# A spectral mixing kernel and its feed-forward layer: the second batch's inputs loaded before weight block 5, and two of three row loads moved to GpSimd's queue

## The chip, the cores and the metric

The kernel runs on one core of a Trainium2 chip. The time is the device time of one execution in microseconds. The kernel before took 2579.2 us in the median of three runs (2575.68 to 2580.06).

## The reference

The input x has 8 batches of 3008 positions and 256 channels. Each channel is filtered in the frequency domain, and the result goes through a feed-forward layer with 2048 hidden units, all in float32. The two weight matrices and the other inputs are given in their own types; the weights are 64-bit floats, which the kernel turns into float32 itself.

```python
X = np.fft.rfft(x, axis=1)
Y = X * (filt_r + 1j * filt_i)[None, :, :]
y = np.fft.irfft(Y, n=x.shape[1], axis=1)       # (8, 3008, 256)
t = y.reshape(8 * 3008, 256)
h = t @ w_in                                    # (24064, 2048)
out = (h * (1 / (1 + np.exp(-h)))) @ w_out      # (24064, 256)
```

## The kernel before

The main part is the feed-forward layer. It runs in 384 steps: 48 pieces of tokens by 8 pairs of hidden blocks. Each step has 14 matmuls of 128x128 by 256 (lines 756 and 819); they use a seven-product scheme, so the weights stand in SBUF in seven combinations (w_t, filled by place_weights and combine_weights). While the steps of one batch run, the Fourier transforms of the next batch are put between them by a list of due times. That list holds for everything after step 0; what comes before is written out by hand, in the order in which each engine is to do it, and the change lies there.

This opening does four things at once, because nothing can start before them:

1. Weights. load_weights (lines 926 and 929) loads block j of 16 as two DMAs of 256 KB on SP's queue. VectorE and ACT turn the 64-bit words into float32 (bits, converted, rounded) and VectorE places the products in w_t (placed). Blocks 0 to 3 are loaded first, 4 to 8 later, 9 just before the main loop.
2. Tables and filters. The transform's tables d_t, e_t and wi_t and the filters come by SP's, ACT's and POOL's queues (POOL is the profile's name of GpSimd, whose DMAs go by a queue of their own).
3. The first batch's transform: stage1_first, then for each of six groups g a forward (line 467), a product with the filters, and an inverse (line 527, matmuls into pc). rows_first (line 541) copies the two results of a group from PSUM, by ACT, and for groups 4 and 5 one of them by VectorE, and stores each with a 256-KB DMA (line 543) into a DRAM tile d2. The store is issued by the engine that copied, or by SP where VectorE copied. Twelve stores in all.
4. The transform's last stage reads d2 in another order. load_t4_rows(k) (line 571) loads part k in two DMAs of 256 KB each. Part 0 needs the stores of groups 0 and 1, part 1 of groups 2 and 3, part 2 of groups 4 and 5. The rows go to a part of w_t that the weights don't need yet. stage3(g) for g = 0 to 3 (line 586, matmuls into pd) needs all three parts, and the main loop begins with its results.

The second batch's first two pieces are also begun here: load_two loads 768 KB into x_all (line 277, SP's queue), after the first batch's stage 1 has read x_all for the last time; stage1 (line 345) multiplies it. Between this and stage 3, idle_wide(n) (line 1055) puts n matmuls whose result nobody reads.

Engines work in their own order and wait for each other by semaphores. A DMA is issued by the engine named in the call, in its order, so an issue that must wait holds up what follows on that engine.

Of the kernel before, what the change touches and what calls it, by code (L numbers as in the profile page):

```python
# [170 lines left out]
def kernel(  # L171
# [9 lines left out]
    nc = tc.nc  # L181
# [69 lines left out]
    def bank(b, name, spare=None):  # L251


        if early[0] is None and spare in ("x", "yz"):
            return xps.tile([128, 2, C], FP32, name=name, tag=spare)
        if early[0] is None and spare is not None:
            return accps.tile([128, 2, C], FP32, name=name, tag=f"a{spare}")
        if early[0] is None:
            return fps.tile([128, 2, C], FP32, name=name, tag="f")
        early[0] += 1  # L260
        k = early[0] % 8
        if k < 2:
            return fps.tile([128, 2, C], FP32, name=name, tag="f")
        if k > 5:
            return xps.tile([128, 2, C], FP32, name=name, tag="x" if k == 6 else "yz")
        return accps.tile([128, 2, C], FP32, name=name, tag=f"a{k - 2}")
# [459 lines left out]
    def combine(eng, out, in0, in1, op):  # L726
        eng.tensor_tensor(out=out, in0=in0, in1=in1, op=op)  # L727
# [176 lines left out]
    def load_weights(j, queue=None):  # L904

        if j in (8, 11, 12, 13):
            pool, tag = (t4pool, "t4") if j in (11, 12) else (upool, "u")
            raw = pool.tile([128, 2, 512], U32, name=f"raw_{j}", tag=tag)
        else:

            if j in (0, 2):
                t = ypool.tile([128, 2, HALF], FP32, name=f"raw_{j}", tag="y")
                raws.setdefault("tiles", []).append(t)
                raws["at"] = t.rearrange("p a n -> p (a n)").bitcast(U32)[:, 0:2048]
                raws["y"] = raws["at"]
                raws.setdefault("first", raws["at"])
            elif j == 4:
                raws["at"] = spool.tile([128, 2048], U32, name=f"raw_{j}", tag="s")
            elif j == 6:
                raws["at"] = gpool.tile([128, 2048], U32, name=f"raw_{j}", tag="g")  # L920
            elif j in (9, 14):
                raws["at"] = raws["y"]
            at = 1024 * (j in (1, 3, 5, 7, 10, 15))
            raw = raws["at"][:, at:at + 1024].rearrange("p (w n) -> p w n", w=2)
        queue = queue or nc.sync
        queue.dma_start(
            out=raw[:, 0].rearrange("p (a n) -> p a n", a=2),
            in_=moe_w_in.bitcast(U32)[:, 256 * j:256 * j + 256].rearrange("(a p) n -> p a n", p=128))
        queue.dma_start(out=raw[:, 1], in_=moe_w_out.bitcast(U32)[128 * j:128 * j + 128, :])
        raws[j] = raw  # L930

    def bits_of_weights(*js):

        for j in js:
            words = raws[j].rearrange("p w (n t) -> p (w n) t", t=2)
            if j in (6, 7):

                room = w_t.rearrange("p j c w n -> p (j c w n)")[:, (7168, 13056)[j - 6]:][:, 0:1024].bitcast(U32)
                e, m = room[:, 0:512], room[:, 512:1024]
            elif j in (0, 1, 4, 5):  # L940
                if "scratch" not in raws:
                    raws["scratch"] = gpool.tile([128, 4, 512], U32, name="scratch", tag="g")
                e, m = (raws["scratch"][:, 2 * (j % 2) + i] for i in range(2))
            else:
                e = zpool.tile([128, 512], U32, name=f"e_{j}", tag="z")
                m = ppool.tile([128, 512], U32, name=f"m_{j}", tag="p")
            lo, hi = words[:, :, 0], words[:, :, 1]
            ef, mf = e.bitcast(FP32), m.bitcast(FP32)
            ends = (lo, hi) if j in (2, 3, 6, 7) else (m, e)
            raws[j] = lo, hi, e, m, ef, mf, ends[0].bitcast(FP32), ends[1].bitcast(FP32), ends[1]  # L950
            v.tensor_scalar(out=e, in0=hi, scalar1=20, scalar2=0x7ff,
                            op0=ALU.logical_shift_right, op1=ALU.bitwise_and)
            v.tensor_scalar(out=m, in0=hi, scalar1=0xfffff, scalar2=None, op0=ALU.bitwise_and)
# [42 lines left out]
    def combine_weights(jp, part=None, eng=None):  # L996

        eng = eng or v

        def w(c):  # L1000
            return w_t[:, jp, c]
        if part != 1:
            combine(eng, w(S1), w(S3), w(A22), ALU.add)
            combine(eng, w(S2), w(S1), w(A11), ALU.subtract)
        if part != 0:
            combine(eng, w(S3), w(A11), w(S3), ALU.subtract)
            combine(eng, w(S4), w(A12), w(S2), ALU.subtract)

    def weights(*js, queue=None):
        for j in js:  # L1010
            if wide:
                load_weights(j, queue)

    def bits(*js):
        if wide:
            bits_of_weights(*js)
# [34 lines left out]
    def idle_wide(n, ps=None, rhs=None):  # L1051

        ps = ps or bank(0, "idle")
        for _ in range(n):
            nc.tensor.matmul(out=ps[:, 0], lhsT=wx_t, rhs=wide_rows if rhs is None else rhs,
                             start=True, stop=True)
# [4 lines left out]
    part, second = spectral(0), spectral(1)  # L1061
# [13 lines left out]
    nc.scalar.dma_start(out=d_t[:, 16:NS], in_=d_dram[:, 16:NS])  # L1075
    nc.scalar.dma_start(out=e_t[:, 2:NG], in_=e_dram[:, 2:NG])
    nc.sync.dma_start(out=wi_t, in_=ws_dram.ap())
    weights(4, 5, 6, 7)

    signed = []  # L1080
    for i in range(2):
        t = typool.tile([128, 2, 2, 2, 128], FP32, name=f"signed_{i}", tag="ty")
# [26 lines left out]
    for k in range(16):  # L1109
        part["stage1_first"](k, 2)  # L1110
        if k in whole:
            part["stage1_first"](whole[k], 3)
    second["load_two"]()
    weights(8)
    part["forward"](0, fill=4)
    placed(0, 1)
    for g in range(1, 4):
# [8 lines left out]
    def inverse(g):  # L1126
        part["inverse_first"](g)
        part["rows_first"](g)
# [15 lines left out]
    for k in range(2):  # L1144
        part["add"](NG - 1, k)
    bits(4, 5)
    inverse(4)
    combine_weights(0)
    inverse(5)
    bits(6, 7, 8)  # L1150
    for k in range(2):
        part["load_t4_rows"](k)
    part["load_t4_rows"](2)
    converted(4, 5)
    placed(2, 3)
# [11 lines left out]
    gp.tensor_copy(out=gate, in_=w_t[:, 4, A11, 0, 0:1])  # L1167
    for u in range(2):
        second["store_rows"](u)
    idle_wide(16)  # L1170
    for g in range(4):
        part["stage3"](g)
    nc.sync.dma_start(out=wi_t, in_=wi_dram.ap())
# [93 lines left out]
```

## Time and profile before

| what | value |
|---|---|
| median of three runs | 2579.2 us |
| the profiled execution | 2579.25 us |
| its span, first to last instruction | 2577.4 us |
| TensorE busy over the span | 2553.1 us, 99% |
| mean granted TensorE clock | 0.995 |
| stage 3 (line 586) of the opening starts | 69.10 us |
| first matmul of the main loop (line 756) | 76.94 us |

Busy time of TensorE counts its matmuls; PEld is its loading of weights, beside the matmuls. A "q" behind an engine's name means its issuing side. Times in the views are microseconds from the start of the span. In the windows view, a row has the stretch, its length, the busy time (and number of instructions) of TensorE, its weight loads, VectorE, ACT and POOL, then the granted clock as a share of full speed, the mean busy share of the 16 DMA engines, and GB/s moved. In the timeline, a row has start, duration, engine, line, operation, output and inputs with shapes, the number of instructions, and in brackets the idle time before and what ended it. In the chain of waits, a row has start, duration and what the chain went through.

### The profile page before, as it was taken

The page shows a single profiled execution, that of the slowest core. Times are in us where ns is not written, and L with a number is a line of the kernel's source. Part 1 is how long each engine was busy: PE and PEld are TensorE (multiplying, and loading weights), DVE is VectorE, ACT ScalarE, POOL GpSimd, SP SyncE. Part 2 cuts the span into 40 slices and gives each one's busy share as a digit, 9 for nine tenths or more (in the row PEclk, how much of TensorE's full clock was granted, in tenths as well). Part 3 has the DMA queues.
Part 4 walks back from the last instruction along what each step waited for, and adds up shares of the span by engine and source line. Part 5 has one row for each costly group of instructions (what it writes and reads, how often), then busy time and mean ns, then how long its engine had stood idle before and what let it go on. Part 6 is the DMA issues. An engine that isn't in the chain of part 4 may idle for free.

```text
span 2577.4 us, 47850 instructions
## 1 busy us (share of the span) xinstructions
PE 2553.1 (99%) x18714; PEld 2196.6 (85%) x18714; DVE 1664.4 (65%) x3589; ACT 1090.4 (42%) x3019; POOL 430.3 (17%) x688
## 2 busy tenths in 40 slices
PE   8999999999999999999999999999999999999998
PEld 6688888888888888888888888888888888888987
DVE  7766666676666666666666676666666666555554
ACT  3544444444444444444444444444444444444443
POOL 4212111111122111311121111211121112101101
PEclk9899999999999999999999999999999999999999
DMA  9522232222223222322233122331232211200011
GB/s 291 158 60 52 70 79 63 60 68 72 59 64 69 70 65 55 79 71 67 59 70 80 49 66 59 79 80 46 66 86 64 68 41 34 59 18 16 9 17 16
DMA packets 198554, 171.06 MB, mean 66 GB/s; under 512 B 122068, under 2 KB 173380, under 8 KB 197348
## 3 DMA queue, kind: packets, MB, share of 16 engines
q1 hardware_dynamic: 176056, 117.06, 19.9%
q0 software_dynamic: 17344, 45.70, 5.6%
q10 hardware_dynamic: 4928, 5.24, 0.7%
q8 instruction: 147, 2.41, 0.4%
q14 instruction: 79, 0.65, 0.1%
HBM read 96.07 MB, written 81.26 MB: 69 GB/s over the span
## 4 chain that ended last, share of the span: by engine, by line
PE 96%; DMA 2%; DVE 0%; ACT 0%; issue 0%; SPq 0%; ACTq 0%; DVEq 0%
PE acc L819 44%; PE px L756 26%; PE pyz L756 19%; PE pd L586 3%; PE pb L467 2%; PE pc L510 2%; PE pf L434 1%; DMA filt<-in_filt_i_dram 0%; PE pa L354 0%; DMA w_t<-in_x_dram 0%; DMA d_t<-d_tbl 0%; PE pa L345 0%; DMA x_all<-in_x_dram 0%; DMA d<-q 0%; DMA w_t<-d 0%; DMA t<-d 0%
## 5 line engine op out<-in xcount | busy, mean ns | idle before, releaser
L819 PE MATMUL acc<-g,w_t 128*128 128x256 f32 (+1 forms) x5376 | 1509.2, 375 | 0.4 <-DVE g L727 0.4
L819 PEld LDWEIGHTS acc<-g,w_t 128*128 128x128 f32 x5376 | 1021.6, 190 | 115.7 <-DVE g L727 0.8
L727 DVE TENSOR_TENSOR g<-pyz,abc 128x256 f32<-128x256 f32 (+1 forms) x1152 | 480.0, 417 | 621.6 <-ACT abc L777 356.2
L727 DVE TENSOR_TENSOR g<-g 128x256 f32<-128x256 f32 (+3 forms) x1152 | 599.4, 520 | 196.7 <-ACT g L760 183.5
L756 PE MATMUL px<-ty,w_t 128*128 128x256 f32 (+1 forms) x2304 | 679.4, 377 | 1.1 <-ACT abc L771 0.6
L760 ACT ACTIVATE g<-g 128x256 f32<-128x256 f32 (+1 forms) x1152 | 472.9, 410 | 250.2 <-DVE g L727 250.2
L727 POOL TENSOR_TENSOR s<-s 128x256 f32<-128x256 f32 (+1 forms) x329 | 255.0, 792 | 1417.5 <-DVE s L839 1321.0
L756 PEld LDWEIGHTS px<-ty,w_t 128*128 128x128 f32 x2304 | 432.7, 190 | 65.5 <-issue 6.2
L756 PE MATMUL pyz<-y,w_t 128*128 128x256 f32 (+1 forms) x1536 | 454.0, 377 | 0.0
L756 PEld LDWEIGHTS pyz<-y,w_t 128*128 128x128 f32 x1536 | 283.9, 190 | 47.6 <-DVE g L727 6.8
L771 ACT COPY abc<-px 128x256 f32<-128x256 f32 (+1 forms) x384 | 141.3, 368 | 372.9 <-PE px L756 372.9
L777 ACT COPY abc<-px 128x256 f32<-128x256 f32 (+1 forms) x384 | 141.5, 369 | 339.0 <-PE px L756 338.1
L760 ACT ACTIVATE g<-px 128x256 f32<-128x256 f32 (+1 forms) x384 | 145.8, 380 | 300.9 <-PE px L756 300.8
L756 PE MATMUL px<-y,w_t 128*128 128x256 f32 (+1 forms) x768 | 232.7, 385 | 0.8 <-DVE y L600 0.8
L756 PE MATMUL pyz<-ty,w_t 128*128 128x256 f32 (+1 forms) x768 | 225.8, 376 | 0.3 <-DVE g L727 0.2
L756 PEld LDWEIGHTS px<-y,w_t 128*128 128x128 f32 x768 | 140.4, 190 | 33.0 <-DVE y L606 5.3
L756 PEld LDWEIGHTS pyz<-ty,w_t 128*128 128x128 f32 x768 | 144.5, 190 | 19.2 <-DVE g L727 1.5
L764 ACT COPY abc<-px 128x256 f32<-128x256 f32 (+1 forms) x384 | 135.4, 353 | 52.7 <-PE px L756 52.7
L586 PEld LDWEIGHTS pd<-wi_t,t 48*64 48x64 f32 x3840 | 61.1, 135 | 25.1 <-ACT g L760 16.4
L446 POOL DMA_DIRECT2D d<-tf x144 | 71.6, 504 | 29.2 <-DVE tf L442 29.2
L839 ACT COPY s<-acc 128x512 f32<-128x512 f32 (+1 forms) x94 | 54.2, 577 | 47.6 <-PE acc L819 47.4
L869 DVE STREAM_TRANSPOSE o<-s 128x256 f32<-128x256 f32 x192 | 73.9, 423 | 0.4 <-issue 0.3
(136 smaller groups left out, 1269.9 us busy)
## 6 DMA issues: line engine op xcount, KB each, us to landing
t<-d SPq DMA_DIRECT2D x120, 192.0 KB
t<-d SPq DMA_DIRECT2D x84, 256.0 KB
d<-q POOLq DMA_DIRECT2D x84, 256.0 KB, 2.7
out_dram<-o SPq DMA_DIRECT2D x636, 32.0 KB
d<-tf POOLq DMA_DIRECT2D x144, 96.0 KB, 3.2
xr<-in_x_dram SPq DMA_DIRECT2D x6, 1472.0 KB
x_all<-in_x_dram SPq DMA_DIRECT2D x72, 96.0 KB
x_all<-xr SPq DMA_DIRECT2D x72, 96.0 KB
```

Source lines behind the costliest of these rows:

```text
L446: nc.gpsimd.dma_start(out=d1[k // 2, :, k % 2, n0:n0 + 4], in_=us["tf"][32 * k:32 * k + NS].rearrange("p q n c -> p (q n) c"))
L467: nc.tensor.matmul(out=ps[k][32 * j:32 * j + 32, ri, :], lhsT=d_t[rows, 4 * g + at, ri, :], rhs=rhs, start=True, stop=True)
L586: nc.tensor.matmul(out=ps[h][c0:c0 + 64, cb, i, :], lhsT=t4[rows, i, 128 * cb + c0:128 * cb + c0 + 64], rhs=wi_t[rows, :], start=True, sto ...
L727: eng.tensor_tensor(out=out, in0=in0, in1=in1, op=op)
L756: nc.tensor.matmul(out=out, lhsT=w_t[:, jp, c, 0], rhs=rhs, start=start, stop=True, skip_group_check=True)
L760: nc.scalar.activation(out=g[:, k, 0:n], in_=g[:, k, 0:n] if src is None else src, func=AFT.Silu)
L764: nc.scalar.copy(out=sums[:, 0, 0:n], in_=xo)
L771: nc.scalar.copy(out=sums[:, 1, 0:n], in_=xo)
L777: nc.scalar.copy(out=sums[:, 2, 0:n], in_=xo)
L819: nc.tensor.matmul(out=acc[pair][i][:, h, 0:n], lhsT=w_t[:, jp, c, 1], rhs=g[:, k, 0:n], start=(jp == 0 and h == 0), stop=last, skip_group ...
L839: copy(out=s[:, 2 * i:2 * i + 2, 0:n], in_=acc[pair][i][:, :, 0:n])
L869: v.transpose(out=o[:, :, h, :], in_=results[pair][:, ((2, 6), (4, 1))[chunk][h], :])
```

## The change

Three things move. The weights' loads of blocks 4 to 8 are split: block 4 stays ahead of the second batch's inputs, blocks 5 to 8 come behind them on SP's queue. Parts 0 and 1 of the row loads go from SP's queue to GpSimd's, and stand earlier in the program. The filling matmuls ahead of stage 3 go from 16 to 12.

```diff
     nc.sync.dma_start(out=wi_t, in_=ws_dram.ap())
-    weights(4, 5, 6, 7)
-
...
+    weights(4)
     second["load_two"]()
-    weights(8)
+    weights(5, 6, 7, 8)
     part["forward"](0, fill=4)
...
     bits(4, 5)
+    part["load_t4_rows"](0, nc.gpsimd)
     inverse(4)
     combine_weights(0)
+    part["load_t4_rows"](1, nc.gpsimd)
     inverse(5)
     bits(6, 7, 8)
-    for k in range(2):
-        part["load_t4_rows"](k)
     part["load_t4_rows"](2)
...
     for u in range(2):
         second["store_rows"](u)
-    idle_wide(16)
+    idle_wide(12)
     for g in range(4):
         part["stage3"](g)
```

## The prediction

> **What bounds the kernel now.** I read the page first, for what fills the span.
>
> ```profile
> PE 2553.1 (99%) x18714; PEld 2196.6 (85%) x18714; DVE 1664.4 (65%) x3589; ACT 1090.4 (42%) x3019; POOL 430.3 (17%) x688
> PEclk9899999999999999999999999999999999999999
> DMA  9522232222223222322233122331232211200011
> ```
>
> TensorE is busy 99% of the span, and after the first slices nothing else limits. DMA is near full only in the first slice (64 us each), and only in the first two does the clock dip. The change touches nothing after that opening stretch, so its price is how much earlier or later the main loop starts. The second view is the chain of waits inside the opening.
>
> ```profile
> 41.42 1.87 PE pc L527 x14
> 43.29 8.54 DMA x_all<-in_x_dram
> ...
> 51.91 0.37 ACTq L543
> ...
> 57.66 4.00 DMA d<-q
> ...
> 62.27 6.70 DMA w_t<-d
> 68.97 0.14 issue
> 69.10 7.12 PE pd L586 x254
> ```
>
> Read from the end: stage 3 (pd) starts at 69.10 because the last row load (part 2) landed at 68.97; that load was issued at 62.27, after the last store of group 5, issued at 57.66, landed at 61.66. The third view is TensorE's timeline over the same time.
>
> ```profile
> 46.38 3.50 PE L527 MATMUL pc<-w_t,signed 64*128 64x256 f32 x29 [0.28 <-ACT q L541]
> ...
> 53.48 3.70 PE L345 MATMUL pa<-x_all,wx_t 96*128 96x512 f32 x8
> 57.01 7.07 PE L1055 MATMUL idle<-d_t,wx_t 96*128 96x256 f32 x32
> 67.84 0.42 PE L586 MATMUL pd<-wi_t,w_t 48*64 48x47 f32 x2 [3.76 <-DMA w_t<-d]
> 69.10 7.07 PE L586 MATMUL pd<-wi_t,w_t 48*64 48x47 f32 x254 [0.84 <-DMA w_t<-d]
> ...
> 201.63 1.15 PE L586 MATMUL pd<-wi_t,t 48*64 48x47 f32 x64
> ```
>
> The second batch's inputs (x_all) are first read at 53.48, though they landed at 51.83: 1.65 us of slack. Fill matmuls run from 57.01 to 64.08, then TensorE waits for part 2. The last view, windows, shows why that load is slow and what the wait does to the clock (columns: busy time of five engines, granted clock, DMA share, GB/s).
>
> ```profile
> 52.00:57.00 5.00, 5.00 (x22) 2.65 (x19) 2.09 (x6) 2.81 (x5) 0.00 (x0) 1.00 1.10 382
> 57.00:62.00 5.00, 5.00 (x25) 4.39 (x24) 5.00 (x15) 4.97 (x10) 0.00 (x0) 1.00 1.19 334
> 64.00:66.00 2.00, 0.08 (x1) 0.00 (x0) 1.97 (x6) 2.00 (x5) 0.00 (x0) 1.00 1.02 246
> 66.00:66.50 0.50, 0.00 (x0) 0.00 (x0) 0.50 (x2) 0.50 (x2) 0.00 (x0) 0.57 0.86 203
> 86.50:87.00 0.50, 0.50 (x3) 0.45 (x3) 0.33 (x1) 0.00 (x0) 0.00 (x0) 0.95 1.09 238
> ```
>
> The DMA engines are full (share about 1.0) all the way: stores of 256 KB at 382 GB/s, 0.69 us each; row loads of 256 KB at 246 GB/s, 1.07 us each (1.15 by the mean distance of their landings). So part 2 is late because transfers stand in line, not because its issue is late. The clock falls to half at about 66.1, 2 us after the last fill matmul, and returns at about 86.5: stage 3 runs cold, 7.12 us against 4 x 1.08 = 4.3 us at the pace of the 64 matmuls at 201.63.
>
> **The change part by part.** The sum is made against the profiled execution's 2579.25 us (span 2577.4, 1.85 around it), which is also the median of the runs within 0.1 us.
>
> *Second batch's inputs ahead of weight blocks 5 to 8.* On SP's queue, the six DMAs of blocks 5 to 7 (two per block) move behind the 768-KB load; block 4's two and block 8's two keep their side of it. The load takes block 5's first slot: issued at 38.49 instead of 43.29. It lasts about 3.5 us on the engines (43.29's neighbour landed at 48.30 by the trace's landing events, it at 51.83), so it lands near 46.5, and TensorE's 53.48 does not notice: gain 0. Blocks 5 to 7 land 3.5 us later, block 5 at about 47.8 instead of 44.3; VectorE opens it at 49.74, 2 us of cover; blocks 6 to 8 are opened from 57.55, over 3 us of cover. SP itself will stand for the eighth of these DMAs until x_all has landed, near 46.5 (the semaphores, below); behind it on SP is nothing before the store at 55.60. The work ahead of the stores is the same bytes in another order, so the stores' landings stay.
>
> But the semaphores in the trace show a second effect. The DMAs of SP and ACT take eight completion semaphores in turn, and an issue waits for the DMA that had its semaphore before. Today ACT's first store (issue 45.32) is eight behind block 5's second half; its sixth store is eight behind x_all, and ACT stands 1.5 us until 51.91. After the change the first store is eight behind block 5's first half (landing 43.7 + 3.5 = 47.2), so ACT stands there 1.9 us with all its copies queued behind it, and the later wait goes away: copies two to five come 1.8 us later, the last ones 0.4 us. TensorE's matmul at 46.38 waits for the second copy, so TensorE comes 1.8 us later through 57.01. VectorE's two copies (54.88, 56.95) wait for the first stores' landings and the weight combines, not for this: SP's last store stays at 57.66. On the end: 0, covered by the fill; the cover is 64.08 - 57.01 = 7 us, and beyond it each us would cost one.
>
> *Fill 16 to 12.* Each takes 7.07 / 16 = 0.44 us, so 1.8 us less of work whose end nobody waits for. With TensorE 1.8 us late, the fill ends again at 64.1; price 0, since the clock is down before stage 3 either way.
>
> *Parts 0 and 1 by POOL's queue.* Four issues leave SP (58.21 to 60.3) and go to POOL, whose last work ended at 48.5 and whose next is at 71.7; about 0.5 us each there (eight L372 issues in 4.07 us). POOL stands in two waits, with only those loads behind it, and they take four of its own eight semaphores, free since 38.2. Part 0 needs groups 0 and 1, stored by 56.05: it can start 2.2 us earlier than today. Part 1 needs group 3, stored at 58.79: today it is issued at 59.13, so nothing is won there. Both now run beside the eight stores that are still under way. Part 0 takes 2 x 1.15 = 2.3 us of full engines and pushes the last store from 61.66 to 63.96. Part 1 follows at about 61.1 plus 1.5 for issue and start; between 0 and 2.3 us of it falls ahead of the last store. I take half, since two queues take turns: last store at 65.1. Part 2 is then issued at once and no longer stands behind four loads. Its second half took 6.70 us from issue; unqueued, from below: 0.53 for the issue of its first half, 2.43 for the 24-KB load of wi_t at 76.24, 1.07 for data, 4.0 us; from above: 0.53 plus 4.5 us, the 384-KB x_all load of 76.62, 5.1 us. I take 4.1, as the line is short by then: landing at 69.2 instead of 68.97.
>
> The ends of this part: best, the POOL loads fit into gaps that the stores leave, the last store stays at 61.66 and part 2 lands at 65.7 (-3.3 us); worst, part 1 falls wholly ahead and part 2 takes 5.1: 63.96 + 2.3 + 5.1 = 71.4 (+2.4 us).
>
> Here the Trainium skill speaks against the change: "DMA: Bandwidth & Descriptors", section "Issuing engines are not separate DMA queues", says that DMAs of all issuers share the same 16 engines and that a second issuer saves only issue time. This trace's share of 1.0 from 52 to 62 agrees; by that rule alone this part would give 0.
>
> The sum: 0 (inputs) + 0 (fill) + 0.2 (parts): 2579.5 us. From 2576.0 to 2581.7 for this case alone.
>
> **The rivals.** *The clock stays up (faster).* TensorE idles 1.21 us before 39.44 without a fall, and 1.99 us before the fall at 66.07. If part 2 lands at the best end, 65.7, the wait after the fill (64.1) is 1.6 us, between these. Then stage 3 costs 4.3 instead of 7.1 (-2.8), and the main loop's first matmuls run warm: the stretch from 77 to 86.5 has 8.4 us of cold matmuls, of which up to 4.2 could go, but they wait for ACT and VectorE in turn, so I take half, 2.1. With -3.3 for the start: -8.2, 2571 us. For it: the DMA rate falls from 382 to 246 as soon as loads run alone, so mixing may pay. Against: shares of 1.0 leave no gaps, and stage 3 itself may be too thin to hold the clock, since it did not bring it back in 7 us.
>
> The Trainium skill, "TensorE: Matmul & The Clock Gate", section "Part 1: The HAM clock gate", puts the fall after an idle window of about 3.4 us; here it came 2 us after the last matmul. By that page a wait of 1.6 us would surely keep the clock.
>
> *POOL's loads starve the stores (slower).* From 32 to 37 us, where POOL's queue and both others ran together, the windows give only 215 GB/s. Eight stores and four loads are 3.15 MB; at that rate they last 14.7 us from 56.05, to 70.7, and part 2 lands at 74.8: +5.8, 2585 us. It is slower by more than 0.2% below 224 GB/s (3.15 MB in the 14.0 us to 70.1). Against: from 57 to 62 large loads and stores mix at 334 GB/s. For: there both came from hardware queues.
>
> *The semaphores are dealt otherwise (no change).* Then ACT does not stand at the first store, the fill ends at 62.3, and TensorE waits 1.8 us longer for the same load: 2579.
>
> **How the numbers follow.** 0.2% (5.2 us) is about what a measurement of this kernel can tell from no change. The forecast and the semaphore rival, both no change, get 0.52; the clock rival 0.27, faster; starving 0.21, slower, which I put above the evidence of 57 to 62 because 215 GB/s is the only row with POOL's queue in the mix. The range runs from the clock case to the starving case: 2571 to 2585, with the clock's own ends (the first steps gaining 0 to 4.2) a little outside.
>
> **What would show it.** In the changed profile: x_all issued near 38.5; ACT's first store near 47.2; the fill ending near 64; POOL's two pairs of issues near 56 and 61; the last store landing near 65 instead of 61.66; stage 3 near 69; clock 0.5 over it. Wrong would be a last store still near 61.7 (loads fit in gaps), a granted clock of 1.0 over stage 3, or stores spread beyond 68.

## The result: slower by 0.16%

The changed kernel took 2582.0 us in the median of 20 runs (2578.4 to 2586.6), the kernel before 2577.6 us in the median of 20 (2573.3 to 2580.1). The ratio is 1.0016, with a 95% interval of 1.0010 to 1.0022: about 4.1 us slower. That lies inside the predicted 2571 to 2585 and within 0.2%, where the forecast was no change; but these 20 runs resolve it, and it is a loss. The profiled execution took 2582.29 us with a span of 2580.5, against 2579.25 and 2577.4.

The page of the changed kernel hardly differs from the one of before: TensorE is busy for 2552.4 us, again 99% of the span. Four matmuls fewer are 8 instructions fewer on TensorE (18706 for 18714), and POOL has 4 more (692 for 688), the row loads. The loss shows in the chain of waits inside the opening:

```profile
37.55 9.69 DMA raw<-in_moe_w_in_dram
...
47.32 0.38 ACTq L543
...
47.74 0.59 ACT q L541
...
48.38 9.85 PE pc L527 x62
...
67.36 4.55 DMA w_t<-d
...
72.05 7.38 PE pd L586 x254
```

The chain now goes from block 5's first half (raw) to ACT's first store, through ACT's copy to TensorE, and only then to the row load. Stage 3 starts at 72.05 instead of 69.10, and the main loop's first matmul (line 756) at 80.14 instead of 76.94. TensorE's timeline says what happened on the way:

```profile
48.38 6.18 PE L527 MATMUL pc<-w_t,signed 64*128 64x256 f32 x29 [3.08 <-ACT q L541]
58.15 3.70 PE L345 MATMUL pa<-x_all,wx_t 96*128 96x512 f32 x8
...
70.60 0.28 PE L586 MATMUL pd<-wi_t,w_t 48*64 48x47 f32 x2 [3.56 <-DMA w_t<-d]
72.05 7.33 PE L586 MATMUL pd<-wi_t,w_t 48*64 48x47 f32 x254 [1.17 <-DMA w_t<-d]
```

TensorE stood 3.08 us for ACT's second copy, and the 29 matmuls behind it took 6.18 us; the same 29 took 3.50 before. The windows give the reason (columns as before: granted clock, DMA share and GB/s are the last three). First the kernel before:

```profile
45.00:51.00 6.00, 5.29 (x44) 4.47 (x46) 6.00 (x14) 3.22 (x6) 3.53 (x6) 1.00 1.00 230
```

Then the changed one:

```profile
45.00:51.00 6.00, 2.92 (x14) 2.19 (x14) 6.00 (x13) 1.76 (x3) 3.94 (x6) 0.67 1.07 363
57.00:62.00 5.00, 5.00 (x20) 2.65 (x17) 4.97 (x15) 3.73 (x8) 0.00 (x0) 1.00 0.92 149
```

The clock averaged 0.67 from 45 to 51 (the trace's clock record has it at 0.5 from 47.0 to 53.8), where before it was 1.00. And from 57 to 62, while POOL's two loads of part 0 (issued at 55.23 and 55.82) ran beside the stores, the DMA engines moved 149 GB/s; before, they moved 334 there. Part 1 was not yet under way: its first load was issued at 63.74, since the store that it needs landed at 63.19.

The span grew by 3.1 us. The 140th matmul of the main loop's line 819 comes at 162.27 us instead of 160.47, so 1.8 of it is the opening: part of its 3 us had come back by then, since the clock was up again at 84.55 and not at 86.55. By its last matmul TensorE is 2.8 us behind, so about 1 us more is lost later, in a loop that the change does not touch; another 0.3 us comes after that matmul. TensorE's waits after 140 us, first before and then after:

```profile
PE pd L586 <- DVE g L727: 0.3, 1, 0.3
```

```profile
PE pd L586 <- issue: 1.4, 2, 0.8
PE pd L586 <- DVE g L727: 0.3, 1, 0.3
```

Each line has what waited, for what, the sum in us, how often, and the longest. Two waits for which this view names nothing ("issue") are new. All idle time of TensorE after 140 us is 2.12 us instead of 0.67; some 0.4 us of these 1.45 came back elsewhere in the loop.

### The profile page after: what moved, and what is told of

The parts are those of the page before. It is cut to its first block, busy times and chain, and to the rows that moved or that the text cites. A ratio compares the mean times of both kernels' runs of the same rounds, so it can differ in the third digit from the quotient of the medians.

```text
span 2580.5 us, 47837 instructions
## 1 busy us (share of the span) xinstructions
PE 2552.4 (99%) x18706; PEld 2196.3 (85%) x18706; DVE 1663.8 (64%) x3589; ACT 1091.5 (42%) x3019; POOL 431.8 (17%) x692
## 4 chain that ended last, share of the span: by engine, by line
PE 96%; DMA 2%; DVE 1%; issue 0%; ACT 0%; ACTq 0%; SPq 0%; DVEq 0%
PE acc L819 44%; PE px L756 26%; PE pyz L756 19%; PE pd L586 3%; PE pb L467 2%; PE pc L510 2%; PE pf L434 1%; DMA raw<-in_moe_w_in_dram 1%; DMA w_t<-in_x_dram 0%; PE pa L354 0%; PE pa L345 0%; DMA filt<-in_filt_r_dram 0%; PE pc L527 0%; DMA d_t<-d_tbl 0%; DVE g L727 0%
```

## The experiments

Two theories stood after the result. A: the order of the loads costs most, through ACT's wait and TensorE's clock. B: the rows on POOL's queue cost most, by pushing the last stores. The later runs brought in a third, C: the shorter fill costs, in the main loop. Every ratio below is against runs of the kernel before on the same chip; the intervals are about 2.3 us to either side, so a difference of two single parts is seldom resolved by time alone, and the positions in the profiles carry the argument. A position comes from one execution, and executions differ: the table e_t, for which ACT's first work in this stretch waits, landed between 40.2 and 45.9 us in these profiles (41.86 before, 41.03 in the change). Where that matters it is said.

**The order alone.**

```diff
-    weights(4, 5, 6, 7)
...
+    weights(4)
     second["load_two"]()
-    weights(8)
+    weights(5, 6, 7, 8)
```

> Only the order of the loads on SP's queue is changed; rows and fill as before. Theory (two losses that add: the order makes ACT's first store stand for its semaphore, TensorE waits 3 us for the copy behind it and its clock falls; the rows on POOL's queue push the stores): ACT's first store is issued near 47.3, TensorE waits about 3 us before the inverse of group 2 and the clock falls to 0.5 there, the last store is issued near 59.4 instead of 57.66, stage 3 starts near 70.6, time +1.5 us (+0.06%). Rival (all of the loss comes from POOL's loads ahead of the stores, the order costs nothing): last store at 57.7, stage 3 near 69.1, time +0.

Measured: 2579.45 us, ratio 1.0007 (0.9997 to 1.0016). TensorE's timeline:

```profile
49.06 6.08 PE L527 MATMUL pc<-w_t,signed 64*128 64x256 f32 x29 [3.05 <-ACT q L541]
72.31 7.21 PE L586 MATMUL pd<-wi_t,w_t 48*64 48x47 f32 x254 [0.70 <-DMA w_t<-d]
```

The same wait, the same cold 29 matmuls, and stage 3 at 72.31, without any load on POOL's queue. ACT's first store was issued at 48.00 and the last store at 59.95 instead of 57.66. It landed 2.3 us after its issue, with the line in front of it empty; but part 2 then stood 7.7 us behind parts 0 and 1. All this is as theory A forecast, stage 3 somewhat later than its 70.6. So theory A is enough for 3 us in the opening, though in time the part gives only 1.8 us (-0.8 to 4.1).

**The rows alone.**

```diff
+    part["load_t4_rows"](0, nc.gpsimd)
     inverse(4)
     combine_weights(0)
+    part["load_t4_rows"](1, nc.gpsimd)
     inverse(5)
     bits(6, 7, 8)
-    for k in range(2):
-        part["load_t4_rows"](k)
     part["load_t4_rows"](2)
```

> Only the rows of parts 0 and 1 go to GpSimd's queue; order and fill as before. Theory of two losses: ACT's first store near 45.3, last store issued near 57.7 but landing near 65 instead of 61.66 because part 0 goes ahead of it, part 2 lands about 5 us later, near 70.2, time +1.2 us (+0.05%). Rival (all of the loss is POOL's loads): last store lands near 66.7, stage 3 near 72, time +4 us (+0.16%).

Measured: 2578.11 us, ratio 1.0001 (0.9992 to 1.0010). TensorE's 29 matmuls start at 46.38 and take 3.50 us, as before, and its timeline goes on:

```profile
68.42 7.07 PE L586 MATMUL pd<-wi_t,w_t 48*64 48x47 f32 x254 [0.53 <-DMA w_t<-d]
```

The last store took 7.43 us (56.19 to 63.63) instead of 4.00, and part 2 took 3.99 (64.30 to 68.29) instead of 6.70: what the stores lose, the last load wins. The earlier stage 3 (68.42 for 69.10) is no gain of the rows: the last store was issued 1.5 us earlier than in the profile of before, and that differs from execution to execution (55.8 to 56.6 in the other five profiles with the order of before). In the six profiles with the order of before, whatever their rows and fill, stage 3 starts between 67.90 and 69.25; in the five with the inputs moved ahead and block 8 on SP's queue it starts between 72.05 and 75.87. So with the order of before, theory B costs nothing that shows, neither its own forecast of 1.2 us nor the rival's 4.

**The whole change, with matmuls that should hold the clock.** In the first half of the inverse of group 2, seven fill matmuls stand ahead of the others.

```diff
+            for _ in range(7 if g == 2 else 0):
+                nc.tensor.matmul(out=ps[0][:, 0], lhsT=wx_t, rhs=wide_rows, start=True, stop=True)
```

> The whole change, and 7 more filling matmuls (3.1 us) in front of the inverse of group 2, where TensorE waited. Theory: the fall of the clock made TensorE 4.7 us late where the wait itself was worth 1.8; with the clock held at 1.0 the inverses end 1.8 to 2 us late only, the last store is issued near 57.7 instead of 59.37, stage 3 starts near 70.3 instead of 72.05, time 1.7 us below the change (+2.4 us over before, +0.09%). Rival (the clock does not matter, ACT's copies set the pace): last store still near 59.4, time as the change, +0.16%.

Measured: 2582.06 us, ratio 1.0017 (1.0008 to 1.0026). This did not test what it was meant to. TensorE's timeline:

```profile
49.41 6.30 PE L522 MATMUL pc<-d_t,wx_t 96*128 96x256 f32 x14 [3.45 <-ACT q L543]
```

In this execution the table e_t landed at 45.93, where it had been 41.03, and ACT's work on it came 5 us later and its first store 2 us later. The fills waited 3.45 us for ACT themselves and then ran at half clock (14 instructions in 6.30 us, 0.90 a matmul instead of 0.44). So the forecast (last store near 57.7, 1.7 us won) was not put to the test, and what the clock alone is worth stays open.

**The whole change, with the inputs one block later.**

```diff
-    weights(4)
+    weights(4, 5)
     second["load_two"]()
-    weights(5, 6, 7, 8)
+    weights(6, 7, 8)
```

> The whole change, but the second batch's inputs are loaded behind weight block 5 instead of ahead of it, so that ACT's first store has block 5's second half as the DMA that used its semaphore before. Theory (the semaphore is what ACT stands for): ACT's first store near 45, its second near 47.5 to 48, TensorE does not wait for the second copy and keeps its clock, the last store is issued near 57.7, time +1 to +2.5 us over before (+0.04 to +0.1%). Rival (ACT stands because the queue is full, whatever the semaphore): first store still near 47, time +0.16%.

Measured: 2581.44 us, ratio 1.0015 (1.0006 to 1.0024). ACT's timeline:

```profile
46.94 0.38 ACTq L543 DMA_DIRECT2D d<-q  x1
...
50.13 0.37 ACTq L543 DMA_DIRECT2D d<-q  x1
50.54 0.59 ACT L541 COPY q<-pc 128x512 f32<-128x512 f32 x1 [2.60 <-DMA x_all<-in_x_dram]
```

By the count of eight, the first store should now stand for block 5's second half and the second for x_all. They landed at 46.86 and 50.05; the stores were issued at 46.94 and 50.13. That is the count of the prediction, and the copies behind wait with them. But the numbers that the theory forecast did not come: it had the first store near 45, no wait of TensorE and a loss of 1 to 2.5 us, while the rival (a full queue holds ACT, whatever the semaphore) had the store near 47 and 0.16%, which is what was measured. What decides for the semaphore is the trace: each DMA's record names its completion semaphore, there are eight in turn, and in all 13 cases in these profiles in which a store of ACT's stood, it was issued 0.07 to 0.08 us after the DMA that had held its semaphore landed. TensorE's two waits were shorter (1.42 and 1.20 us), the clock was at 0.5 from 48.0 to 51.4 only, and still nothing was won: ACT's last store, issued at 58.44, took 10.75 us to land, and stage 3 began at 74.18.

**The whole change, with the fill of before.** `idle_wide(16)` instead of `idle_wide(12)`.

> The whole change, but the fill keeps its 16 matmuls. The order alone gave +1.8 us and the rows alone +0.3, the change +4.1. Theory (the two parts meet: the order makes the last stores late, and POOL's loads then run ahead of them; the fill costs nothing because the wait for part 2 covers it): fill ends near 68.7, stage 3 starts near 72, time as the change, +4 us (+0.16%). Rival (the shorter fill is the missing third loss): time +2.1 us (+0.08%), with a higher granted clock over stage 3.

Measured: 2580.82 us, ratio 1.0011 (1.0002 to 1.0020). The opening was no better (stage 3 at 73.14, main loop's first matmul at 81.22), but TensorE's idle time after 140 us was 0.67 us, exactly as before, and the two waits for "issue" were gone. What four matmuls more or fewer change is thus the main loop, not the opening. The time (+2.8 us, between the theory's 4 and the rival's 2.1) does not tell the two apart.

**The fill of 12 alone.** The kernel before with `idle_wide(12)`.

> The kernel before with 12 filling matmuls, nothing else. Theory (instruction count): the opening as before within 0.5 us, TensorE idles 1 to 2 us after 140 us instead of 0.67, time +1.2 us (+0.05%). Rival (the cover holds and the fill is free, as the prediction had it): idle 0.67, time 0.

Measured: 2579.55 us, ratio 1.0006 (0.9997 to 1.0014). Stage 3 starts at 69.25, the main loop at 77.09, as before. TensorE's waits after 140 us:

```profile
PE pd L586 <- issue: 0.7, 1, 0.7
```

Again a wait for "issue" in the transform's stage 3 within the loop; idle time 1.32 us instead of 0.67. Theory C holds in its place, as forecast, and its size is about 0.4 to 1.5 us of idle time in four kernels with 12 fills (1.09 with block 8 moved, 1.32 here, 1.65 with the inputs one block later, 2.12 in the change).

**A long fill.** The kernel before with `idle_wide(26)`.

> The kernel before with 26 filling matmuls instead of 16, and nothing else changed. Theory (stage 3 is cold because TensorE waits 5 us ahead of it): the fill ends near 68.5, the clock stays 1.0 over stage 3 (4.3 instead of 7.1 us) or falls late in it, time -3 to -6 us (-0.1 to -0.25%). Rival (stage 3's own matmuls are too thin to hold the clock): the clock falls within stage 3, time 0 to -1 us.

Measured: 2577.57 us, ratio 1.0001 (0.9992 to 1.0010). TensorE's timeline:

```profile
67.90 3.47 PE L586 MATMUL pd<-wi_t,w_t 48*64 48x47 f32 x222 [0.64 <-DMA w_t<-d]
```

The fill ran from 55.62 to 67.01. The windows give a clock of 1.00 through stage 3, and the main loop began at 74.11 instead of 76.94. Of these 2.8 us, 1.2 are an earlier start of stage 3, in an execution whose e_t came 1.4 us earlier, and 1.6 the shorter stage 3 itself (5.4 us to its end at 73.32, with a wait of 1.26 inside, for 7.1). The 140th matmul came 2.9 us earlier. Then the loop idled 2.79 us instead of 0.67 (three waits for "issue" in front of line 586's matmuls, 2.1 us), and 2.1 of the gain was spent. In time nothing was left of the 3 to 6 us forecast. **The rows alone with the same fill** gave the same:

> Only the rows on GpSimd's queue, with 26 filling matmuls. If the rows cost nothing and the fill holds the clock, as the kernel before with 26, -3 to -6 us; if stage 3 cannot hold the clock, 0 to -1 us. The fill should end near 68.5, stage 3 start near 68.5 to 69.

Measured: 2578.34 us, ratio 1.0003 (0.9995 to 1.0012); 140th matmul 2.7 us earlier, idle time 2.75 us.

**The whole change, with block 8 moved off SP's queue.** Two DMAs fewer stand ahead of ACT's stores; block 8 goes by POOL's queue, after POOL's additions.

```diff
-    weights(5, 6, 7, 8)
+    weights(5, 6, 7)
...
+    weights(8, queue=nc.gpsimd)
     inverse(2)
```

> The whole change, but weight block 8 is loaded by GpSimd's queue after its additions, so that two DMAs fewer stand on the hardware queues ahead of ACT's first store. Theory (ACT stands for the DMA that had its semaphore eight before): the first store now follows the table load e_t (landed near 41) and is issued near 44.5, the second follows x_all, near 47; TensorE waits less than 1 us for the second copy and its clock does not fall; the last store is issued near 57 and the time is 1.5 to 2.5 us below the change (+0.06 to +0.1% over before). Rival (ACT stands because the queues are full): first store still near 47, time as the change.

Measured: 2581.10 us, ratio 1.0014 (1.0005 to 1.0022). TensorE's timeline, and the chain at the last store:

```profile
45.07 3.50 PE L527 MATMUL pc<-w_t,signed 64*128 64x256 f32 x29 [0.28 <-ACT q L541]
70.60 7.07 PE L586 MATMUL pd<-wi_t,w_t 48*64 48x47 f32 x254 [0.66 <-DMA w_t<-d]
```

```profile
54.72 10.79 DMA d<-q
```

ACT's first store (44.01) no longer stood for block 5, its second did for x_all (issued at 46.18, x_all landed at 46.10), TensorE did not wait, and its 29 matmuls were warm again: that much as the theory forecast, and against the rival's store near 47. Stage 3 came 1.45 us earlier than in the change, but the 1.5 to 2.5 us forecast were not shown in the time (0.9). Yet all stores were issued by 54.72 and the last landed 10.79 us later. From 60 to 62 the engines were still full (share 1.09, 382 GB/s); the next windows show that they were not for the rest:

```profile
62.00:64.00 2.00, 0.00 (x0) 0.00 (x0) 2.00 (x5) 2.00 (x5) 0.00 (x0) 1.00 0.34 124
64.00:66.00 2.00, 0.00 (x0) 0.00 (x0) 1.97 (x6) 2.00 (x4) 0.00 (x0) 0.73 0.03 12
```

From 64 us to the landing of the store at 65.51 hardly anything moved: the mean share of the 16 engines is 0.03.

**The order with block 8 moved, and the rows on SP's queue as before.** The same two edits of the loads as in the last run, made to the kernel before; fill 16.

> The order of the change with weight block 8 on GpSimd's queue after its additions, the rows on SP's queue as before, fill 16. With the rows on GpSimd's queue the last store was issued at 54.7 and landed at 65.5. Theory (POOL's row loads run ahead of the stores): here the last store, issued near 54.7, lands within 5 us, near 59.5, part 2 near 67, stage 3 starts near 67 and the time is 2 us below before (-0.08%). Rival (the stores are late because the line is long, whoever issues the rows): last store lands after 63, time +1 to +3 us.

Measured: 2577.80 us, ratio 1.0000 (0.9991 to 1.0009). The chain at the same place:

```profile
55.24 5.46 DMA d<-q
...
68.31 5.33 PE pd L586 x242
```

The last store took 5.46 us instead of 10.79, and stage 3 began at 68.31 instead of 70.60. The two runs differ in the rows' queue and in the fill; the fill did nothing to the opening when it was changed alone, and e_t, at 41.16, came 0.6 us later than in the last run, which can't be what made it faster. So with early stores theory B costs about 2.3 us in the opening of these two executions, where it cost nothing that shows with the stores of before; the ratios differ by 0.0014, some of which is the fill of 12. ACT's first store (44.62) did not stand, its second stood until x_all had landed (46.81), TensorE waited for neither, and the order of the loads then costs nothing. The gain of 2 us that was forecast did not come: the last store landed at 60.70, near enough to 59.5, but part 2, behind parts 0 and 1, only at 68.06, where 67 was forecast, and by the time nothing was won.

**A long fill without more instructions.** The kernel before; six fill matmuls of 256 columns and ten of 512, 16 in all.

```diff
-    idle_wide(16)
+    fill = bank(0, "idle")
+    idle_wide(6, fill)
+    for _ in range(10):
+        nc.tensor.matmul(out=fill.rearrange("p a c -> p (a c)"), lhsT=wx_t,
+                         rhs=d_t[0:96].rearrange("p s r n -> p (s r n)")[:, 0:512], start=True, stop=True)
```

> The kernel before with 16 filling matmuls as before, but 10 of them 512 columns wide, so that they last as long as 26 while TensorE's instructions stay as many as before. Theory (the number of TensorE instructions ahead of the main loop sets where TensorE must wait for its instructions in front of the small pd matmuls: every kernel with 16 fills idles 0.67 us after 140 us, those with 12 idle 1.1 to 2.1, those with 26 idle 2.8): idle after 140 us 0.67, the opening 2.9 us shorter as with 26, time -3 us (-0.12%). Rival (the longer fill itself costs the main loop its 2 us): idle near 2.8, time 0 to -0.5 us.

Measured: 2575.80 us, ratio 0.9993 (0.9984 to 1.0002). Idle time after 140 us: 0.67 us, as the theory of the instruction count has it. But in the profiled execution (2578.28 us, one of the two highest of 11) the clock fell all the same, after two waits of about 1 us:

```profile
67.77 0.28 PE L586 MATMUL pd<-wi_t,w_t 48*64 48x47 f32 x2 [1.07 <-DMA w_t<-d]
69.01 6.97 PE L586 MATMUL pd<-wi_t,w_t 48*64 48x47 f32 x254 [0.96 <-DMA w_t<-d]
```

So its main loop began at 76.75, only 0.2 us earlier than before, and the 3 us forecast are not shown: the interval runs from a gain of 4.1 us to a loss of 0.5.

**The last two together.** The order with block 8 moved, rows on SP's queue, and this long fill.

> The order of the change with block 8 on GpSimd's queue and rows on SP's, and the fill lengthened without a change in the number of instructions (6 matmuls of 256 columns and 10 of 512). Theory (the opening's gain and the main loop's instruction count add up): fill from 56.3 to 67.7, part 2 at about 68, TensorE's wait under 1.5 us in front of stage 3, the clock held, main loop's first matmul near 73 to 74 instead of 75.84, idle after 140 us 0.67; about 2.5 us below before, 2575, ratio 0.999. Rival (a short wait and the thin matmuls of stage 3 drop the clock anyway, as in the run with the long fill alone): stage 3 cold, 7.0 us, first main matmul near 76, time within 1 us of before, ratio 1.000.

Measured: 2575.67 us, ratio 0.9996 (0.9987 to 1.0005). Seven of the 11 runs lie from 2574.3 to 2575.7, four from 2577.7 to 2580.8, and the profiled execution is one of the four (2579.77). What made it late is the table e_t again, landed at 45.36:

```profile
48.92 0.67 PE L527 MATMUL pc<-w_t,signed 64*128 64x256 f32 x2 [3.55 <-ACT q L541]
```

ACT did not stand for a semaphore here: its first store came 3.45 us after e_t, as in the kernel before (3.46). TensorE waited 3.55 us all the same, the 29 matmuls behind took 5.13, and the clock record has 0.5 from 49.8 to 53.2. Stage 3, behind the long fill, ran warm, but the main loop began at 79.71, where 73 to 74 was forecast. Idle time after 140 us is 0.67 us once more. The run also says that e_t can land 4 us later with x_all issued well behind it (34.02 and 38.95), so an x_all close to it, as in the run with the seven fills (34.19 and 34.62), is not needed for that. In both, e_t was itself issued late (30.6 to 33.1 in the other profiles) and took 11.3 to 11.7 us to land (9.2 to 10.3 in the others). What is behind either stays open. No version was shown to beat the kernel before; the two with the long fill of 16 come nearest.

## Why the prediction was right in its answer and wrong in two steps

The forecast of no change within 0.2% held, and the time lies within 2571 to 2585. The sum did worse: it puts the change 0.3 us above its base of 2579.25, and 4.1 us above the base of 2577.6 were measured; the case's own range, 2576.0 to 2581.7, was just missed by 2582.0. So the answer held by the width of "no change", not by the sum, and two of the terms set at zero were not zero. Of the signs, ACT's first store (47.32), POOL's first pair (55.23) and the clock of 0.5 over stage 3 came near what was said; the fill's end (67.0 for 64), POOL's second pair (63.74 for 61), the last store's landing (66.69 for 65) and stage 3 (72.05 for 69) came some 2 to 3 us late.

*Inputs ahead of blocks 5 to 8: mechanism right, its price wrong.* x_all was issued at 37.16 and landed at 46.78; ACT's first store was issued at 47.32 against the predicted 47.2, behind block 5's first half. That is the semaphore effect as predicted, and moving the inputs by one block moved ACT's stands as the count says. The step that failed is "SP's last store stays at 57.66. On the end: 0, covered by the fill". TensorE came later not by 1.8 us but by 4.7: 2.0 by the wait (48.38 for 46.38), and 2.7 because the wait dropped the clock (6.18 for 3.50). VectorE's copies, which the prediction had waiting only for stores and weights, were then waiting for TensorE. VectorE's timeline before:

```profile
54.88 0.69 DVE L541 COPY q<-pc 128x512 f32<-128x512 f32 x1 [3.70 <-DMA d<-q]
```

And in the changed kernel:

```profile
56.59 0.69 DVE L541 COPY q<-pc 128x512 f32<-128x512 f32 x1 [5.02 <-PE pc L527]
```

This copy and the next came 1.7 us later than before (56.59 and 58.66 for 54.88 and 56.95), and the last store was issued at 59.37. The fill covered TensorE's own lateness, but not the stores that hang on TensorE's results. That the order alone, with rows and fill as before, moves stage 3 to 72.31, and that it does not do so once TensorE waits no more (68.31), shows this step. That ACT's wait did it, and not the load ahead of block 5 in some other way, rests on the releases of the timelines and on the semaphores above. How much of it the clock has, apart from the wait, was not separated.

*Fill 16 to 12: right in the opening, wrong after it.* The fill ended at 67.0 and TensorE then waited 4.7 us, so its end was indeed awaited by nobody. But the price of 0 left out the main loop: after 140 us TensorE idles 0.67 us in every kernel with 16 fill matmuls, 1.1 to 2.1 in those with 12, 2.8 in those with 26. This is the other part of the loss, 1.45 us in the change. Putting the 16 back took the ratio from 1.0016 to 1.0011. Order, rows and fill, each alone, add up to 3.6 us (1.8, 0.3 and 1.5) of the 4.1; none of the three is resolved by time alone.

*Parts 0 and 1 by POOL: close in the sum, by luck.* From its issue the last store was to take 7.44 us (57.66 to 65.1) and took 7.32. But it was put together from 2.3 us for part 0 at full engines and half of part 1. Part 1 was issued at 63.74 and hardly any of it can lie ahead of a store that landed at 66.69, as its own first completions came at 66.49. The delay belongs to part 0 alone, at a price that the sum did not have: between 57 and 62 its 16-KB packets took 1.84 us each in the median, while the engines moved 149 GB/s at a share of 0.92; the row packets that SP's queue carried in the kernel before took 1.1 us. Part 2, 4.1 us after that, took 5.22 (66.69 to 71.91), of which 0.67 is the issue of its first half. Against the predicted 69.2, part 2's landing is 2.7 us late: 1.7 by the late issue above, -0.1 by the store, 1.1 by part 2 itself. Alone this part moved the time by 0.01%, and stage 3 by no more than executions differ, within its predicted ends.

*The semaphore rival* is refuted by ACT's first store at 47.32, and *the clock rival* for this kernel by stage 3's 7.33 us at half clock; what it needed, part 2 landing at 65.7, did not come either (71.91). With 26 fills the clock did stay up, but stage 3 took 5.4 us, not 4.3: at full clock a wait of 1.26 us appears inside it (what for, stands at the end of this document). The rival's gain was sized too large. *The starving rival* had the right mechanism: 149 GB/s from 57 to 62, below its 215, and stores of over 10 us in two kernels. It erred in how long that lasts: the rate was back at 373 GB/s from 62 to 64, and the stores were all landed by 66.7.

The Trainium skill's rule in "DMA: Bandwidth & Descriptors", section "Issuing engines are not separate DMA queues", which spoke against the change, agrees with the rows moved alone: no gain from a second issuer. It does not say what the run with early stores shows, that the second issuer can cost.

## What to carry to other kernels

An earlier load is not free when it shares a small set of completion semaphores with other queues: count which later DMA takes over its semaphore, and whose engine stands there. A wait put on TensorE is priced with the clock that it may drop and with everything that waits for TensorE's results, not only with the work that ends the stretch. A filling matmul has a price beyond its time, so a saved or added one has to be looked for in the whole span.

## What was not expected of the hardware

*A transfer ends with the slowest of 16 engines.* In the run with block 8 moved, the 16 completions of the last store came from 60.67 to 65.51. The packets still on the way after 63.5 were, by the trace, ten 1-KB ones of the store (0.046 us each) that alternate with four 16-KB ones of POOL's loads (0.61 us each), by their order on a single engine, while the mean share of the engines was 0.03 to 0.34. With the rows on SP's queue the last store took half as long. Each of POOL's four loads has 16 such packets, one for each engine if they were spread evenly; why one engine was so far behind stays open. So "the engines are full and transfers stand in line", as the prediction read the share of 1.0, holds for most of the stretch before (0.48 to 0.71 in some half microseconds after 62.5) and not for this mix. The Trainium skill, "DMA: Bandwidth & Descriptors", section "Queues, rings and completion order", says that an engine takes turns between queues packet by packet. The alternation agrees; an estimate by that rule and these two durations: on an engine where both are waiting, a queue of 16-KB packets gets 13 times the time of one of 1-KB packets (0.61 over 0.046).

*TensorE's clock falls by stretches of 3.41 us, not by a wait's length alone.* It fell in the change (a wait of 3.08 us), with the order alone (3.05), and with e_t late (3.45 and 3.55), and the 29 matmuls behind, 3.5 us when warm, took 5.1 to 6.2 us (with the seven fills, these took 6.30 us for 3.1). It also fell after waits of 1.07 and 0.96 us ahead of stage 3 with the long fill, and after 1.42 and 1.20 us with the inputs one block later. With the order and block 8 moved, TensorE idled 3.75 and 0.89 us ahead of stage 3, and the clock was down for 3.41 us only (68.37 to 71.79). In the clock records of all 14 profiles, the stretches between the opening and the loop are multiples of 3.41 us (3.41 to 20.48), and where they begin differs from execution to execution. In the 3.41 us ahead of the 24 falls between 25 and 110 us TensorE was busy for 0 to 1.93 us; with 2.10 us or more no such stretch ended in a fall, and one with 1.84 us passed without. So it counts how a wait lies against these stretches, which an estimate from a single profile can't know. Why stage 3's thin matmuls, busy throughout, left the clock at 0.5 in nine of these kernels and had it back after 3.41 us in the one just named stays open. The Trainium skill, "TensorE: Matmul & The Clock Gate", section "Part 1: The HAM clock gate", puts the fall after an idle window of about 3.4 us that runs freely; the lengths agree, but windows that were idle only in part were enough here.

*The number of TensorE's instructions in the opening goes with waits at 650 to 2240 us.* With 18714 instructions the idle time after 140 us was 0.67 us in all seven kernels, whatever the length of the fill and whatever else was changed. With 18706 it was 1.09 to 2.12 in four, with 18734 2.75 and 2.79 in two; with 18720, in the run that was to hold the clock, 0.9 us of waits for "issue" were added. The new waits stand in front of line 586's matmuls, and the chain of waits names nothing that ends them. The DMA records do. The page of every run has this row (packets, MB, share of the engines' time):

```profile
q8 instruction: 147, 2.41, 0.4%
```

These are TensorE's instructions coming in: packets of 16 KB, one for every 256 instructions of the matmuls and weight loads together, so 64 bytes for each. All 13 new waits after 140 us, and four like them inside stage 3 of the opening (the 1.26 us with 26 fills is one), end 2.4 to 2.8 us after such a packet starts and 1.3 to 1.6 us after it has landed; in the change the packets start at 652.18 and 2234.94 and the waits end at 654.79 and 2237.52. So by these times TensorE waits there for its own instructions. That a different number of instructions in the opening shifts these packets' ends onto small matmuls fits this, but no run placed a packet's end on purpose.
